# Attention's first steps in an order of their own, one expert's weights rounded a step later, the next expert's loads behind the last store of token rows

## Chip, cores and metric

The kernel runs on one core of one Trainium2 chip. The metric is device time in microseconds (us): 325.03 is the median of three runs, which lay between 324.36 and 325.7. Engines are abbreviated as in the profile: PE is TensorE (matmuls), PEld its weight loads, DVE VectorE, ACT ScalarE, POOL GpSimd, SP SyncE, which here only issues transfers. PEq, SPq and so on are the engines' instruction queues.

## Reference

Three layers run one behind the other on 2 batches of 768 tokens, all in 32-bit floats:

```python
# 1. attention with decay: 8 heads of 64; kv_state is carried along the sequence
out[:, :, sl] = ((qb @ kb.T) * Dmask) @ vb + (qb * lam_pow) @ kv_state
kv_state = lam_block * kv_state + (kb * rev_pow).T @ vb
...
# 2. mixture of 8 experts (512 -> 1024 -> 512), one expert for each token
logits = x @ w_gate
e = argmax(logits) if s == 0 or sigmoid(x @ w_local) < 0.5 else prev_e
out[b, s] = softmax(logits)[e] * (relu(x @ w1[e]) @ w2[e])
...
# 3. mixing: a causal depthwise filter of 5 taps gates a projection
gate = sigmoid(conv5(x, conv_w))
out = (gate * (x @ w_val)) @ w_out
```

A token that keeps its expert takes that of the token before it, so the choice runs along the sequence.

## The kernel before

**Attention** goes through 12 chunks of 128 tokens, 0 to 11, six of each batch. The instruction order of all engines is written out by hand in it (L534 to L690): a call such as `scores(2, 0)` issues its instructions on their engine at that place, and each engine then keeps that order. `load_qk` (L82) loads of chunk g, by SP, either the queries and keys for the scores (`qk0`, 512 KB) or the keys and values by token (`qk1`, 512 KB), or a half of one. On PE, `scores(g, half)` (L288) makes four heads' scores, `mix_state` (L309) multiplies queries with the carried state, `mix` (L321) scores with values, `next_state` (L350) makes the new state, `turned` (L370) turns the attention's result to rows of tokens and multiplies it with the gate's weights `wgl_sb`. On DVE, `mask` (L303) multiplies the scores with the decays `dm`; `keys_rest` (L281) and `keys` (L276) scale the keys, on DVE and on ACT; `queries` (L263) scales queries by powers `lq` that `powers` (L120) makes. `mixed` (L329) is ACT's copy of the result; `decay` (L335) and `keep_state` (L358) bring the state on. Ahead of all, `warm` (L529) multiplies zeros on PE.

The choice of the experts trails the attention by one to three chunks (`logits`, `choice`, `kept`, `experts`, `one_hots`, `counted`, `ranks`, `index_factors`, `indices`). `softmax(g)` (L430) ends a chunk: SP stores its 128 rows of 512 values and 8 softmax weights to `xd` in DRAM.

**The experts** run one after the other, 0 to 7. Every 32-bit weight is rounded to a part `whi` (ACT, `split_hi`, L194) and a rest `wlo` (DVE, `split_lo`, L199), and three of four products of parts are summed. Expert 0's eight weight tiles (four of `w1`, four of `w2`, 512 KB each) are loaded during attention by `load_next` (L186); the first four and a half are rounded in it by `first_hi` (L251) and `first_lo` (L256), in halves. The raw tiles, their parts and the `qk` tiles share one pool, `w4`, of 27 buffers. Expert 0's rows are placed by matmuls from what lies on the chip (`place`, L509; `early_split` rounds them), those of experts 1 to 7 are gathered from `xd`: `x_fetch` (L812) issues two indirect transfers of 128 rows on POOL, once `all_indices` (L699) has written the slots `idx`. Then `x_turn` (L828) turns each half on PE, `up` (L853) multiplies with `w1`, `down` (L870) with `w2`, and `down_few` (L880) does the few tokens above 128. In that time the matrices of layer 3, 64-bit values in the input, are loaded by `load64` (L233) and brought to 32 bits by DVE and POOL in `from64_a` (L208, its lines L217 to L226), one 512 KB tile beside each expert.

What the order around the change says of SP, at attention's end:

```python
        softmax(g0)
        load_next(4)
        load64(0)
...
        inverse(g1)
        softmax(g1)
        first_lo(4, HALF[1])
```

`g0` and `g1` are the last two chunks, 10 and 11. In the loop over the chunks before, rounding comes at step s as `first_hi((s - 3) // 2, HALF[(s - 3) % 2])` and `first_lo((s - 4) // 2, HALF[s % 2])`.

Of the kernel before, what the change touches and what calls it, by code (L numbers as in the profile page):

```python
# [44 lines left out]
def fused_kernel(ctx, tc, qkv, lam, wgl, w1, w2, wv, cw, wo, out, dbg=None):  # L45
# [58 lines left out]
    with tc.manual_schedule(engines={mybir.EngineType.SP, mybir.EngineType.DVE}):  # L104
        load_qk(0, slice(0, 1))
        load_qk(0, slice(1, 2))
        load_qk(1, slice(0, 2))
        load_qk(0, slice(2, 4))
        nc.sync.dma_start(wgl_sb, wgl)
        load_qk(1, slice(2, 4))  # L110
        load_qk(2, slice(0, 2))
        load_qk(2, slice(2, 4))
        nc.vector.memset(ones, 1.0)
        nc.vector.tensor_copy(ident16, ident)
        nc.vector.tensor_copy(identr, ident)

        for h in range(H):
            nc.vector.tensor_tensor_scan(dm[:, h, :], lam_sb[:, h:h + 1].to_broadcast([P, P]), last_first, 0.0,
                                         op0=MUL, op1=ADD)

    def powers():

        for hp in range(HP):
            nc.vector.tensor_tensor_scan(lq[:, hp, :], lam_sb[:, H + hp:H + hp + 1].to_broadcast([P, P]), ones, 1.0,
                                         op0=MUL, op1=MUL)
# [40 lines left out]

    nc.scalar.mul(thr_x, zero[:, 0:1], 1.0)
    nc.scalar.dma_start(xd[0:1, 0:XW].rearrange("o (a n) -> (o a) n", a=4), zero[0:4, 0:XW // 4])

# [117 lines left out]

    def scores(g, half, early=False):  # L288
        t = qk_t[g, 0]

        if half == 0 and early:
            rt = ps_1.tile([P, 2, HP, P], F32, name="rt", tag="rt")
            ps_t[g] = [rt[:, rh] for rh in range(2)]
        elif half == 0:
            ps_t[g] = [ps_s.tile([P, HP, P], F32, name=f"ps{rh}", tag=f"ps{rh}") for rh in range(2)]
        for hp in (2 * half, 2 * half + 1):
            for rh in range(2):
                r = slice(rh * 64, rh * 64 + 64)
                c0 = (hp % 2) * P
                nc.tensor.matmul(ps_t[g][rh][:, hp, :], t[r, half, 256 + c0:256 + c0 + P], t[r, half, c0:c0 + P],  # L300
                                 start=True, stop=True)

    def mask(g):  # L303
        ps = ps_t.pop(g)
        sm_t[g] = at_p.tile([P, 2, HP, P], F32, name="sm", tag="sm")
        for rh in range(2):
            nc.vector.tensor_tensor(sm_t[g][:, rh], ps[rh], dm[:, rh * HP:(rh + 1) * HP, :], op=MUL)

    def mix_state(g):  # L309
# [25 lines left out]
    def decay(g):  # L335
        if 0 < g % NC < NC - 1:
            sd_t[g] = sd = at_p.tile([P, HP, D], F32, name="sdec", tag="sdec")
            for hp in range(HP):
                nc.scalar.activation(sd[:, hp, :], state[g][:, hp, :], AF.Copy, scale=lq[:, hp, P - 1:P])
# [18 lines left out]
    def keep_state(g):  # L358
        if g in st_t:
            state[g + 1] = sn = at_p.tile([P, HP, D], F32, name="state", tag="state")  # L360
            if g % NC == 0:
                nc.vector.tensor_copy(sn, st_t.pop(g))
            else:
                nc.vector.tensor_tensor(sn, sd_t.pop(g), st_t.pop(g), op=ADD)
# [169 lines left out]
    with tc.manual_schedule(engines=order_a):  # L534
        warm(10)
        scores(0, 0)
        scores(0, 1)
        warm(6)
        mask(0)
        keys(0)  # L540
        load_qk(3)
        load_qk(4)
        scores(1, 0, True)
        scores(1, 1, True)
        mix_state(0)
        mix(0, 0)
        mix(0, 1)
        mixed(0)
        mask(1)
        keys_rest(0)  # L550
        powers()
        next_state(0)
        warm(2)
        keep_state(0)
        queries(1)
        keys(1)
        keys_rest(1)
        scores(2, 0)
        turned(0)
        for s in range(2, NT):  # L560
            g1, g2, g3 = s - 1, s - 2, s - 3
            last = s == NT - 1
            if s < NT - 3:
                load_qk(s + 3)
            if s in (2, 4, 6, 8):
                load_next()
# [30 lines left out]
            kept(g2)  # L597
            if 3 <= s < 11:
                first_hi((s - 3) // 2, HALF[(s - 3) % 2])
            keys(s, range(2))  # L600
# [10 lines left out]
            if last:  # L611
                softmax(g2)
                parts_hi(g2)
                first_hi(4, HALF[0])
            one_hots(g2)
            if last:
                first_hi(4, HALF[1])
            keys_rest(s)
            keys(s, range(2, HK))
            if s == NT - 2:  # L620
                softmax(g2)
            if s >= 4:
                first_lo((s - 4) // 2, HALF[s % 2])
            if g3 >= 0 and not last:
# [19 lines left out]
        place(ge, (0,))  # L644
        first_lo(4, HALF[0])
        experts(g0)
# [9 lines left out]
        softmax(g0)  # L656
        load_next(4)
        load64(0)
        place(ge, (1,))
        logits(g1)  # L660
        choice(g1)
        token_rows(g1)
        ranks(g0)
# [20 lines left out]
        softmax(g1)  # L684
        first_lo(4, HALF[1])
        place(g1)
        early_split()
        index_factors(ge)
        index_factors(g0)
# [663 lines left out]
```

## Time and profile before

| | before |
|---|---|
| median of three runs | 325.03 us (324.36 to 325.7) |
| the profiled execution | 324.66 us |
| its span, first to last instruction | 322.9 us |
| busy: PE, PEld, DVE, ACT, POOL | 97%, 86%, 81%, 64%, 27% |
| granted TensorE clock | 1.00 |
| memory traffic over the span | 225 GB/s |

The profile shows one execution. Its span leaves out 1.8 us around the first and the last instruction. A busy share is an average over attention (0 to about 75 us), experts (to about 250) and mixing, which have different limits. The chain of waits follows the work that ended last back to the start: it tells which engine's time the kernel consists of.

### The profile page before, as it was taken

The numbers are of one execution on the slowest core, as the hardware profiler recorded it, in microseconds if no ns is written. First come the engines' busy times: TensorE is split into PE (matmuls) and PEld (weight loads), VectorE is DVE, ScalarE is ACT, GpSimd is POOL, SyncE is SP. The second block draws the span as 40 slices with busy tenths as digits, with TensorE's granted clock in tenths as the row PEclk, the third lists the DMA queues.
The fourth block names the chain that finished last, engine by engine and source line by source line (L and its number), as shares of the span: only waits on it lengthen the run. The fifth ranks groups of instructions, "written<-read, shape, count | busy, mean of one in ns | idle before, by whom it ended". The sixth has DMA issues, their size and how long they took to land.

```text
span 322.9 us, 7304 instructions
## 1 busy us (share of the span) xinstructions
PE 314.0 (97%) x2714; PEld 276.8 (86%) x2714; DVE 261.0 (81%) x561; ACT 208.2 (64%) x519; POOL 87.3 (27%) x113
## 2 busy tenths in 40 slices
PE   8899999999979999999999999999999999999995
PEld 3688888889859889899798897988987989989984
DVE  5688899987968979959989799697756799977970
ACT  1589799976638646756576666865646666764741
POOL 7000000200645550550554516525234201020000
PEclk9999999999999999999999999999999999999999
DMA  7999899376599769599599399994304402221102
GB/s 214 376 406 318 298 376 292 150 205 256 180 295 368 285 222 384 202 294 367 215 316 399 120 361 366 304 400 155 96 20 129 125 26 73 102 90 66 63 37 106
DMA packets 27400, 73.09 MB, mean 226 GB/s; under 512 B 3799, under 2 KB 8157, under 8 KB 27357
## 3 DMA queue, kind: packets, MB, share of 16 engines
q1 hardware_dynamic: 24756, 65.09, 56.0%
q0 software_dynamic: 2304, 7.42, 7.5%
q8 instruction: 25, 0.41, 0.5%
q14 instruction: 19, 0.15, 0.1%
q10 hardware_dynamic: 296, 0.03, 0.1%
HBM read 57.79 MB, written 14.73 MB: 225 GB/s over the span
## 4 chain that ended last, share of the span: by engine, by line
PE 89%; DMA 5%; DVE 3%; ACT 1%; issue 1%; POOL 0%; SPq 0%; ACTq 0%
PE ph L862 24%; PE py L876 17%; PE pv L1021 11%; PE py L1047 10%; PE py L886 6%; PE ps L300 4%; PE po L326 3%; DMA xr<-xd,idx 3%; DMA qk<-in_qkv_dram 2%; PE rt L375 2%; PE po L318 2%; PE sp L355 1%; PE px L835 1%; PE rt L378 1%; PE rt L380 1%; PE pt L975 1%
## 5 line engine op out<-in xcount | busy, mean ns | idle before, releaser
L202 DVE TENSOR_TENSOR wlo<-wraw,whi 128x1024 fp32r<-128x1024 f32 (+1 forms) x69 | 85.4, 1264 | 12.9 <-ACT whi L197 12.9
L862 PE MATMUL ph<-xh,whi 128*128 128x240 f32 x512 | 87.2, 276 | 0.0
L862 PEld LDWEIGHTS ph<-xh,whi 128*128 128x128 f32 x512 | 77.4, 189 | 2.0 <-issue 1.5
L862 PE MATMUL ph<-xh,wlo 128*128 128x240 f32 x256 | 69.9, 274 | 0.0
L197 ACT CAST whi<-wraw 128x1024 fp32r<-128x1024 f32 (+1 forms) x69 | 65.3, 988 | 0.7 <-DVE wlo L202 0.7
L876 PE MATMUL py<-whi,hh 128*128 128x512 f32 x176 | 56.5, 392 | 0.0
L862 PEld LDWEIGHTS ph<-xh,wlo 128*128 128x128 f32 x256 | 48.4, 189 | 0.0
L1007 DVE SCALAR_TENSOR_TENSOR gt<-yt,cw_sb,gt 128x256 f32<-128x256 f32 x96 | 39.0, 481 | 1.1 <-ACT gt L999 1.1
L865 ACT ACTIVATE hh<-ph 128x480 fp32r<-128x480 f32 x32 | 18.3, 572 | 33.1 <-PE ph L862 32.7
L876 PEld LDWEIGHTS py<-whi,hh 128*128 128x128 f32 x176 | 33.1, 188 | 6.7
L1021 PEld LDWEIGHTS pv<-yh,wv_t 128*128 128x128 f32 x288 | 35.2, 192 | 0.7 <-ACT gt L999 0.4
L1021 PE MATMUL pv<-yh,wv_t 128*128 128x256 f32 x288 | 35.7, 284 | 0.0
L876 PE MATMUL py<-wlo,hh 128*128 128x512 f32 x88 | 34.4, 391 | 0.0
L1047 PE MATMUL py<-wo_t,gh 128*128 128x512 f32 (+1 forms) x156 | 34.1, 376 | 0.0
L226 POOL TENSOR_TENSOR f64a<-f64a,f64s 128x512 f32<-128x512 f32 (+1 forms) x9 | 18.2, 2027 | 55.6 <-DVE f64s L225 55.5
L1047 PEld LDWEIGHTS py<-wo_t,gh 128*128 128x128 f32 x156 | 27.4, 188 | 5.0
L867 DVE SCALAR_TENSOR_TENSOR hh<-ph,hh 128x480 fp32r<-128x480 f32 x32 | 20.9, 653 | 8.5 <-ACT hf L866 8.4
L815 POOL DMA_INDIRECT xr<-xd,idx x14 | 19.9, 1420 | 10.7 <-DVE hh L867 7.7
L876 PEld LDWEIGHTS py<-wlo,hh 128*128 128x128 f32 x88 | 16.5, 188 | 3.1
L886 PE MATMUL py<-wraw,hf 128*64 128x256 f32 x160 | 18.4, 382 | 0.0
L280 ACT ACTIVATE kd<-qk,dm 128x64 f32<-128x64 f32 x40 | 11.5, 343 | 7.8 <-DMA qk<-in_qkv_dram 7.8
L494 POOL DMA_INDIRECT xr<-xd,idx x2 | 2.1, 1052 | 52.0 <-ACT kp L443 51.7
(201 smaller groups left out, 516.4 us busy)
## 6 DMA issues: line engine op xcount, KB each, us to landing
wraw<-in_w_dram SPq DMA_DIRECT2D x64, 512.0 KB, 6.5
qk<-in_qkv_dram SPq DMA_DIRECT2D x23, 512.0 KB, 8.4
ys<-yo SPq DMA_DIRECT2D x16, 256.0 KB, 3.4
xd<-xtok SPq DMA_DIRECT2D x12, 260.0 KB, 3.6
ys<-warm_sb SPq DMA_DIRECT2D x24, 128.0 KB, 1.9
out_dram<-oo SPq DMA_DIRECT2D x11, 256.0 KB, 2.0
wraw<-in_w_val_dram SPq DMA_DIRECT2D x4, 512.0 KB, 6.6
wraw<-in_w_out_dram SPq DMA_DIRECT2D x4, 512.0 KB, 9.0
```

Of the source, the lines that this page charges most:

```text
L197: nc.scalar.copy(w[1][:, cs], w[0][:, cs])
L202: nc.vector.tensor_tensor(w[2][:, cs], w[0][:, cs], w[1][:, cs].bitcast(F32), op=SUB)
L226: nc.gpsimd.tensor_tensor(a.bitcast(F32), a.bitcast(F32), s.bitcast(F32), op=ADD)
L815: nc.gpsimd.indirect_dma_start(xr[:, t, :], None, xd, bass.IndirectOffsetOnAxis(ap=idx[:, 2 * e + t:2 * e + t + 1], axis=0))
L862: nc.tensor.matmul(ph[:, fi, :], w1_t[e][k][1 + a][:, f * P:(f + 1) * P], xh[b][:, k].rearrange("p t n -> p (t n)")[:, 0:C1], start=first, ...
L865: nc.scalar.activation(hh[:, 0, :, 0:C1], ph, AF.Relu)
L867: nc.vector.scalar_tensor_tensor(hh[:, 1, :, 0:C1], ph, 0.0, hh[:, 0, :, 0:C1].bitcast(F32), op0=ALU.max, op1=SUB)
L876: nc.tensor.matmul(py, hhs[f // 2][:, a, f % 2, t * P:(t + 1) * P], w2_t[e][f // 2][1 + b][:, (f % 2) * DM:(f % 2 + 1) * DM], start=(n == ...
L886: nc.tensor.matmul(py[i * NW:(i + 1) * NW, 0:DM // 2], hf[:, f, :], w2_t[e][f // 2][0][:, (f % 2) * DM + i * DM // 2:(f % 2) * DM + (i + 1 ...
L1007: nc.vector.scalar_tensor_tensor(gt[:, k, :], yt_t[b, k][:, c0 + j:c0 + j + 256], cw_sb[:, k, j:j + 1], gt[:, k, :], op0=MUL, op1=ADD)
L1021: nc.tensor.matmul(pv[:, mi, :], wv_t[:, a, k * DM + m * P:k * DM + (m + 1) * P], yh[b][:, k, :], start=first, stop=last)
L1047: nc.tensor.matmul(po, gh[a][:, k, t * P:(t + 1) * P], wo_t[:, b, k * DM + cs.start:k * DM + cs.stop], start=(i == 0), stop=(i == 11))
```

## The change

It has three parts. The first steps of attention are written out in another order, with chunk 0's values and keys loaded ahead of chunk 1's scores input, narrower masks for chunks 0 and 1 (`mask_half`), fewer warm-ups (8 and 3 in place of 10, 6 and 2), the first state copied by ACT, and chunk 1's state decayed by POOL. The rounding of expert 0's weights in the loop comes a step later. Expert 1's first four loads and the first 64-bit tile are issued behind the last `softmax`.

```diff
@@ loads ahead of the loop
         load_qk(0, slice(0, 1))
         load_qk(0, slice(1, 2))
+        load_qk(0, slice(3, 4))
+        load_qk(0, slice(2, 3))
         load_qk(1, slice(0, 2))
-        load_qk(0, slice(2, 4))
-        nc.sync.dma_start(wgl_sb, wgl)
         load_qk(1, slice(2, 4))
...
-    def powers():
-        for hp in range(HP):
+    def powers(hps):
+        for hp in hps:
...
+    nc.scalar.dma_start(wgl_sb, wgl)
...
+    def mask_half(g, half):
+        if half == 0:
+            sm_t[g] = at_p.tile([P, 2, HP, P], F32, name="sm", tag="sm")
+        hs = slice(2 * half, 2 * half + 2)
+        for rh in range(2):
+            nc.vector.tensor_tensor(sm_t[g][:, rh, hs], ps_t[g][rh][:, hs],
+                                    dm[:, rh * HP + 2 * half:rh * HP + 2 * half + 2, :], op=MUL)
...
     def decay(g):
         if 0 < g % NC < NC - 1:
             sd_t[g] = sd = at_p.tile([P, HP, D], F32, name="sdec", tag="sdec")
+            if g == 1:
+                nc.gpsimd.tensor_tensor(sd, state[g], lq[:, :, P - 1:P].to_broadcast([P, HP, D]), op=MUL)
+                return
...
     def keep_state(g):
...
-            if g % NC == 0:
+            if g == 0:
+                nc.scalar.copy(sn, st_t.pop(g))
+            elif g % NC == 0:
                 nc.vector.tensor_copy(sn, st_t.pop(g))
@@ the order
-        warm(10)
+        warm(8)
         scores(0, 0)
         scores(0, 1)
-        warm(6)
-        mask(0)
-        keys(0)
+        mask_half(0, 0)
+        mask_half(0, 1)
+        warm(3)
         load_qk(3)
         load_qk(4)
-        scores(1, 0, True)
-        scores(1, 1, True)
+        load_next()
+        powers((0, 1))
         mix_state(0)
         mix(0, 0)
         mix(0, 1)
         mixed(0)
-        mask(1)
         keys_rest(0)
-        powers()
+        keys(0)
+        powers((2, 3))
+        scores(1, 0)
+        scores(1, 1)
+        queries(1)
+        turned(0, (0, 1))
+        mask_half(1, 0)
+        mask_half(1, 1)
         next_state(0)
-        warm(2)
         keep_state(0)
-        queries(1)
+        turned(0, (2, 3))
         keys(1)
         keys_rest(1)
+        decay(1)
...
+        mix_state(1)
+        mix(1, 0)
+        mix(1, 1)
+        next_state(1)
...
         scores(2, 0)
-        turned(0)
-        for s in range(2, NT):
+        scores(2, 1)
...
+        for s in range(3, NT):
...
@@ rounding, in the loop
-            if 3 <= s < 11:
-                first_hi((s - 3) // 2, HALF[(s - 3) % 2])
+            if s > 3:
+                first_hi((s - 4) // 2, HALF[s % 2])
...
-                first_hi(4, HALF[0])
             one_hots(g2)
-            if last:
-                first_hi(4, HALF[1])
...
-            if s >= 4:
-                first_lo((s - 4) // 2, HALF[s % 2])
+            if s > 4:
+                first_lo((s - 5) // 2, HALF[(s - 5) % 2])
@@ behind the loop
         place(ge, (0,))
-        first_lo(4, HALF[0])
+        first_lo(3, HALF[1])
...
         softmax(g0)
-        load_next(4)
-        load64(0)
         place(ge, (1,))
         logits(g1)
         choice(g1)
+        first_hi(4, HALF[0])
...
         softmax(g1)
-        first_lo(4, HALF[1])
+        load_next(4)
+        load64(0)
+        first_lo(4, HALF[0])
         place(g1)
         early_split()
+        first_hi(4, HALF[1])
+        first_lo(4, HALF[1])
         index_factors(ge)
```

**SP, the first loads.** `qk_105` is chunk 0's scores input, in two halves. Before, `qk_108` is chunk 1's scores input and `qk_110` chunk 0's keys and values:

```order
L88 DMA qk_105<-in_qkv_dram 128x512 x2
L88 DMA qk_108<-in_qkv_dram 128x1024
L88 DMA qk_110<-in_qkv_dram 128x1024
L109 DMA wgl_sb<-in_wgl_dram 128x36
L88 DMA qk_113<-in_qkv_dram 128x1024
```

Now `qk_108` is chunk 0's values and keys and `qk_111` chunk 1's scores input:

```order
L88 DMA qk_105<-in_qkv_dram 128x512 x2
L88 DMA qk_108<-in_qkv_dram 128x512 x2
L88 DMA qk_111<-in_qkv_dram 128x1024
L88 DMA qk_113<-in_qkv_dram 128x1024
L88 DMA qk_115<-in_qkv_dram 128x1024
```

Chunk 1's scores input moves behind chunk 0's values and keys, and the gate's weights leave this queue.

**PE, from chunk 0's scores on.** The scores of chunk 1 stand ahead of the mixing (`po`) and state update (`sp`) of chunk 0 before:

```order
L300 MATMUL rt<-qk_108 128x128 x8
L326 MATMUL po<-sm,qk_110 64x128 x8
L355 MATMUL sp<-qk_110,kd 64x64 x8
L531 LDWEIGHTS warm_sb
L531 MATMUL pidx<-warm_sb 128x512
```

Now the mixing of chunk 0 comes first, then chunk 1's scores (`ps_243`, `ps_244`), then the turn and the state update:

```order
L332 MATMUL po<-sm,qk_108 64x128 x8
L298 MATMUL ps_243<-qk_111 128x128
L298 MATMUL ps_244<-qk_111 128x128
...
L386 MATMUL rt<-wid,xt 128x137 x2
L364 MATMUL sp<-qk_108,kd 64x64 x8
L389 MATMUL rt<-wgl_sb,xt 128x9
L391 MATMUL rt<-ident,xt 128x128
...
L324 MATMUL po<-qs,state 64x128 x8
L332 MATMUL po<-sm,qk_113 64x128 x8
L364 MATMUL sp<-qk_113,kd 64x64 x8
```

The mixing and state update of chunk 1 now follow at once, with chunk 2's scores behind them; two warm-ups between are gone.

**SP, the end of attention.** `xd` is the store of a chunk's rows, `wraw` a weight tile, `in_w_val_dram` the 64-bit matrix. Before, five loads stand ahead of the last store:

```order
L433 DMA xd<-xtok 128x520 x4
L191 DMA wraw<-in_w_dram 128x1024 x4
L237 DMA wraw_1373<-in_w_val_dram 128x1024
L433 DMA xd<-xtok 128x520
L237 DMA wraw_1688<-in_w_val_dram 128x1024
```

Now all five follow it:

```order
L444 DMA xd<-xtok 128x520 x5
L192 DMA wraw<-in_w_dram 128x1024 x4
L238 DMA wraw_1427<-in_w_val_dram 128x1024
L238 DMA wraw_1684<-in_w_val_dram 128x1024
L192 DMA wraw<-in_w_dram 128x1024 x4
```

The second 64-bit tile and the next four weight tiles stay behind them, in the same order.

## Rows read from the trace of the kernel before

**Rows 1.** The page, part 4: the chain that ended last, by engine.

```profile
PE 89%; DMA 5%; DVE 3%; ACT 1%; issue 1%; POOL 0%; SPq 0%; ACTq 0%
```

**Rows 2.** Chain of waits, 0 to 24 us: start us, us, what.

```profile
8.98 1.19 PE rt L300 x16
...
11.87 0.68 PE sp L355 x14
...
13.19 0.71 PE ps L300 x8
...
19.97 0.65 PE ps L300 x8
```

**Rows 3.** Timeline, 0 to 14 us: start, us, engine line op, tiles, count, [idle before].

```profile
1.26 4.45 PE L531 MATMUL pidx<-warm_sb 128*128 128x512 f16 x10 [1.26 <-DVE warm_sb L78]
...
7.11 1.47 PE L531 MATMUL pidx<-warm_sb 128*128 128x512 f16 x6
...
10.54 1.07 ACT L280 ACTIVATE kd<-qk,dm 128x64 f32<-128x64 f32 x4 [7.79 <-DMA qk<-in_qkv_dram]
```

**Rows 4.** Chain of waits, 72 to 116 us.

```profile
77.11 0.08 DVE idx L703
...
82.84 8.44 DMA xr<-xd,idx
...
95.47 10.95 PE ph L862 x96
...
111.93 0.64 PE px L835 x8
```

**Rows 5.** Timelines of POOL, 74 to 86, and PE, 88.9 to 92 us.

```profile
81.03 1.50 POOL L815 DMA_INDIRECT xr<-xd,idx  x1 [7.72 <-DVE hh L867]
...
89.25 0.46 PE L835 MATMUL px<-identr,xr 128*128 128x128 f32 x4
91.33 0.54 PE L835 MATMUL px<-identr,xr 128*128 128x128 f32 x4 [1.62 <-DMA xr<-xd,idx]
```

**Rows 6.** Timeline of SP, 66 to 74 us (issues, not transfers).

```profile
68.34 1.82 SPq L191 DMA_DIRECT2D wraw<-in_w_dram  x4
...
71.89 0.33 SPq L433 DMA_DIRECT2D xd<-xtok  x1
```

**Rows 7.** DMA issues at 3.1, 67.5, 68.3, 68.7, 71.8, 100.1 us: KB, us to landing.

```profile
qk<-in_qkv_dram SPq DMA_DIRECT2D x1, 512.0 KB, 8.6
...
xd<-xtok SPq DMA_DIRECT2D x1, 260.0 KB, 2.2
...
wraw<-in_w_dram SPq DMA_DIRECT2D x1, 512.0 KB, 4.6
...
wraw<-in_w_dram SPq DMA_DIRECT2D x2, 512.0 KB, 5.0
...
xd<-xtok SPq DMA_DIRECT2D x1, 260.0 KB, 8.4
...
xr<-xd,idx POOLq DMA_INDIRECT x1, 9.6
```

**Rows 8.** Timeline of DVE, 80 to 97 us.

```profile
81.62 0.42 DVE L217 TENSOR_SCALAR f64a<-wraw 128x512 uint32<-128x512 uint32 x1
...
90.36 0.69 DVE L837 TENSOR_TENSOR xh<-px,xh 128x512 fp32r<-128x512 f32 x1 [0.38 <-ACT xh L836]
...
93.13 2.16 DVE L202 TENSOR_TENSOR wlo<-wraw,whi 128x1024 fp32r<-128x1024 f32 x1
```

**Rows 9.** Line L226 over the run: min/median/max ns, first and last start.

```profile
L226 POOL TENSOR_TENSOR f64a<-f64a,f64s x9: 226/2207/4462, 92.9 to 237.1; 128x512 f32<-128x512 f32 x8, 128x20 f32<-128x20 f32 x1
```

**Rows 10.** Timelines of DVE and PEld, 74 to 76.2 us.

```profile
74.05 0.67 DVE L475 TENSOR_SCALAR ixa<-iotah,rk 128x256 f16<-128x256 f16 x3
...
75.44 0.22 PEld L481 LDWEIGHTS <-ixa 128*128 128x128 f16 x6
```

**Rows 11.** Windows: us, busy by engine (PE, PEld, DVE, ACT, POOL), PEclk, DMA share, GB/s.

```profile
89.70:91.30 1.60, 0.01 (x1) 0.00 (x0) 0.97 (x2) 0.58 (x1) 0.00 (x0) 1.00 1.00 332
```

More of the change, by code (lines that the diff above doesn't have):

```diff
@@ L115, in fused_kernel @@
         nc.vector.tensor_copy(identr, ident)
-        for h in range(H):
+        for h in (0, 1, HP, HP + 1, 2, 3, HP + 2, HP + 3):
             nc.vector.tensor_tensor_scan(dm[:, h, :], lam_sb[:, h:h + 1].to_broadcast([P, P]), last_first, 0.0,
                                          op0=MUL, op1=ADD)
-    def powers():
-        for hp in range(HP):
+    def powers(hps):
+        for hp in hps:
             nc.vector.tensor_tensor_scan(lq[:, hp, :], lam_sb[:, H + hp:H + hp + 1].to_broadcast([P, P]), ones, 1.0,
@@ L286, in keys_rest, with scores @@
                 dm[:, HK:H, P - 1:P].to_broadcast([P, H - HK, D]), op=MUL)
-    def scores(g, half, early=False):
+    def scores(g, half):
         t = qk_t[g, 0]
[L291 to L294, printed above, removed]
+        if half == 0:
             ps_t[g] = [ps_s.tile([P, HP, P], F32, name=f"ps{rh}", tag=f"ps{rh}") for rh in range(2)]
@@ L307, in mask @@
             nc.vector.tensor_tensor(sm_t[g][:, rh], ps[rh], dm[:, rh * HP:(rh + 1) * HP, :], op=MUL)
+    def mask_half(g, half):
+        if half == 0:
+            sm_t[g] = at_p.tile([P, 2, HP, P], F32, name="sm", tag="sm")
[3 more added lines that the diff above has]
+                                    dm[:, rh * HP + 2 * half:rh * HP + 2 * half + 2, :], op=MUL)
     def mix_state(g):
@@ L548, in fused_kernel @@
         mixed(0)
-        mask(1)
         keys_rest(0)
-        powers()
+        keys(0)
[6 more added lines that the diff above has]
+        mask_half(1, 1)
         next_state(0)
-        warm(2)
         keep_state(0)
-        queries(1)
+        turned(0, (2, 3))
         keys(1)
         keys_rest(1)
-        scores(2, 0)
-        turned(0)
-        for s in range(2, NT):
+        decay(1)
+        logits(0)
+        choice(0)
+        shift(0)
+        exponents(0)
+        token_rows(0)
+        mix_state(1)
+        mix(1, 0)
+        mix(1, 1)
+        next_state(1)
+        choice_turned(0, 1)
+        kept(0)
+        mixed(1)
+        queries(2)
+        scores(2, 0)
+        scores(2, 1)
+        keep_state(1)
+        experts(0)
+        mask(2)
+        load_qk(5)
+        inverse(0)
+        keys(2, range(2))
+        turned(1, (0, 1))
+        experts_turned(0)
+        turned(1, (2, 3))
+        scores(3, 0)
+        one_hots(0)
+        keys_rest(2)
+        keys(2, range(2, HK))
+        counted(0)
+        for s in range(3, NT):
             g1, g2, g3 = s - 1, s - 2, s - 3
@@ L564, in fused_kernel @@
                 load_qk(s + 3)
-            if s in (2, 4, 6, 8):
+            if s in (4, 6, 8):
                 load_next()
```

## The prediction

> **What bounds the kernel now.** I read the page first, then the chain of waits, then the timelines around the places where it leaves TensorE (PE), then the DMA issues. The chain's shares say that PE holds 89% of the span and single DMAs 5% [rows 1]. So work taken off other engines is worth nothing unless PE waits for it; what counts is where the chain leaves PE. It does so at two places that the change touches.
>
> The first is the start. PE begins the scores of chunk 1 at 8.98, when their input has landed, and from 13.19 it is on the chain without a gap: 6.78 us later, at 19.97, the second half of chunk 3's scores begins [rows 2]. ScalarE's (ACT's) first key instruction starts at 10.54, having waited for the load behind that one [rows 3].
>
> The second is the end of expert 0. The rows of expert 1 are fetched by two gathers. POOL could issue them once the indices exist (`idx`, at 77.11 + 0.08), but the first goes out at 81.03, the second at 82.84; PE turns the first half at 89.25, waits 1.62 us for the second gather and goes on at 91.33 [rows 4, 5]. POOL's row names VectorE's (DVE's) `hh` as the releaser, which was done long before; the true one is a DMA. SyncE's (SP's) queue shows it: five 512 KB loads go out from 68.34 on, and the last store of token rows at 71.89 behind them [rows 6]. That store took 8.4 us to land, where one issued on an emptier queue took 2.2 [rows 7]: 71.89 + 8.4 = 80.3, and the gathers need every store landed.
>
> **The change, part by part.** *The store ahead of the loads.* The store is issued when the softmax is ready, as before, and now has nothing ahead of it: it lands at 71.89 + 2.2 = 74.1. The gathers then start with the indices, at 77.2 in place of 81.03, the second 1.8 us after the first, at 79.0. Among loads, which is where they now run, a gather took as long as 9.6 us [rows 7]; so the second lands by 88.6, and PE wants it after 89.25. With no wait the two turns take 0.64 us, as for expert 2 [rows 4]; the next PE work starts at 89.25 + 0.64 = 89.89 and not at 91.33 + 0.54 = 91.87: **1.98 us saved**.
>
> What is late next? The five loads, now issued from 72.3, some 3.9 us later. The first took 4.6 us and landed at 72.95; the second, issued 0.45 later, took 5.4 (5.0 is the mean of the two) and landed at 74.2 [rows 6, 7]. At 1.25 us each the fifth came at about 78, and now comes at 82, or at 83.2 if the two gathers' 0.5 MB go between. DVE first reads it at 81.62 [rows 8], so DVE may stall up to 1.6 us, and behind it are queued the last `hh` of expert 0 and the rounding of expert 1's weights. DVE had idled 0.38 us before the first turned half [rows 8], so 1.2 of the 1.6 would be left. It delays the last weight part: without a stall that ends at 90.36 + 2 × 0.65 (the turned halves) + 2.16 = 93.8 [rows 8]; PE starts expert 1 at 95.47 − 1.98 = 93.49 and needs the part after nine matmuls of 10.95 / 96 = 0.11 us [rows 4], at 94.5. So 0.7 us of the 1.2 cost nothing and 0.5 would. I take 0, which any quicker loads give, and keep 0.5 as an end. The weight loads ahead of it are used by ACT from 84.6 on, over 2 us after the last.
>
> *The first steps.* The order of loads is now: the two scores halves of chunk 0, its values, its keys, then chunk 1's scores input. That input has 1 MB ahead of it in place of 0.5 MB, so it lands when the load that ACT waited for did: 10.5. From below its landing is bounded by 9.0, where the same transfer came with 0.5 MB ahead, from above by 3.15 + 8.6 = 11.75, where the load behind both came [rows 2, 7]. I take 10.5, since the bytes ahead are the same. From then on PE is to do chunk 1's scores (1.19), chunk 0's state update (0.68) and all that filled the 6.78 us, in another order [rows 2]; nothing else, as the mixing of chunk 0 now runs before. If nothing waits, that ends at 10.54 + 1.19 + 0.68 + 6.78 = 19.19 and not 19.97. Two waits could open: for ACT's copy of chunk 1's state, under which PE turns the second half of chunk 0, and for DVE's masks of chunk 1, under which PE turns chunk 0 and updates its state. I take 0.1 for both: **0.7 us saved**. At the ends, landing at 9.0 would save 2.2, at 11.75 it would lose 0.5.
>
> *The rest.* Chunk 1's decay on POOL: the same kind of pass over twice the size took 2.2 us, at worst 4.5 [rows 9], so 1.1 to 2.2 here; it starts when the state is there, at about 13.4, and the sum that wants it comes at about 15.7, after the mixing and the next state update: 0. The gate weights on ACT's queue go out earlier than on SP's: 0. Rounding a step later: eight half passes of ACT and of DVE stay, under steps that PE bounds; ACT's two in the last step go, 0 to 0.1 saved. The last DVE half pass (0.67) now runs ahead of the three index factors, which ended at 74.05 + 0.67 = 74.72; PE takes them at 75.44 [rows 10], 0.72 later: 0, at worst 0.1 lost.
>
> **Sum.** 324.66 − 1.98 − 0.7 = 321.98 on the profiled execution (span 322.9, 1.8 around it). That execution stood 0.37 under the median of the three runs, 325.03, so I forecast **322.3**.
>
> **A rule against it.** Between mixing chunk 0 and chunk 1's scores PE will idle for 1 to 1.6 us, after fewer warm-up matmuls. The rows show both levels of its clock: ten warm-ups at the start took 4.45 us, six later ones 1.47, so 0.445 and 0.245 each [rows 3]; the first ran at 1.2 GHz, the others at 2.4. The wait around 89.7 to 91.3 left the granted clock at 1.00, the upper level [rows 11]. The Trainium skill ("TensorE: Matmul & The Clock Gate", section "HAM oscillation — how this bites in real kernels") holds that bursts of matmuls parted by waits for DMA can each start at half clock again. By that rule, an estimate, the sum would be 324.9, for 2.6 us more (worked out below from the rows, as E); the trace does not bear it out for one wait of that length.
>
> **Rivals.** *A: both terms hold* (322.3), chance 0.62. For it: both waits stand on the chain, and behind them PE has no other until 111.
>
> *B: only the gather's term.* The input lands at 11.2 or later, where what follows no longer beats 19.97; two loads of 256 KB in place of one of 512 could do that. 325.03 − 1.98 = 323.05; with the landing at 11.75, 323.55. Against: the bytes ahead are the same. Chance 0.17. The Trainium skill ("DMA: Bandwidth & Descriptors", "Rules for kernel authors") wants transfers of 1 MiB and more, and its section "Anatomy of one DMA — SWDGE (gpsimd) path" gives each some 2 us of fixed cost; paid once more in series, an estimate, that would be a landing at 12.5 and 324.3. The rows show loads of 512 KB that take 4.6 and 5.4 us and land 1.25 apart, so what is fixed overlaps.
>
> *C: only the first steps' term.* The gathers now run beside the 2.5 MB of loads, not after them; if the second needs over 12 us, PE waits as before: 325.03 − 0.7 = 324.3. Against: 9.6 is the longest of the rows. Chance 0.10.
>
> *D: neither*, 325.0, chance 0.06: both of these at once.
>
> *E, slower: the clock falls at the wait ahead of chunk 1's scores.* At half clock PE's work takes twice as long, so half of the time that it stays low is lost. At the program's start it was low from 1.26 to somewhere between 5.7 and 7.1, some 5.2 us; that again costs 2.6 and gives 324.9. Low for all of the 8.6 us to 19.2 it costs 4.3: 322.3 + 4.3 = 326.6. It is slower than before from 5.4 us on. For it: the thinner start. Against: rows 11. Chance 0.05.
>
> **How the numbers follow.** A measurement of this kernel tells about 0.5% from no change, 1.6 us: faster is under 323.4, slower over 326.65. A is faster but for a sliver; of B, whose own range is 322.8 to 323.7, some 0.7; C and D are the same; E and a part of D are slower mostly. Faster 0.62 × 0.98 + 0.17 × 0.7 = 0.73; slower 0.04 + 0.02 = 0.06; same the rest, 0.21. The range: A alone reaches from 321.2 (the input at 9.8, and 0.4 between executions) to 323.2; B to 323.7; C's better half to 324.2. Half of C, D and E are left out, 0.16.
>
> **What would show it.** Right: the last store of rows lands some 2 us after its issue; POOL's first gather for expert 1 starts within 0.2 us of `idx`; PE has no wait at the turn of expert 1's rows; chunk 1's scores start near 10.5 and the second half of chunk 3's near 19.3, at a granted clock of 1.00. Wrong: DVE waiting for the fifth load so long that PE waits in expert 1's first matmuls; chunk 1's scores after 11.2; matmuls at the slow pace after 10 us; or the 2.7 us given back by a wait in a later expert, where PE now has none.

## The result, and the profile after

The changed kernel takes **320.75 us** (median of six runs, 320.41 to 321.69), the kernel before 324.69 us (six runs, 322.91 to 326.06): a ratio of 0.9892, 95% interval 0.9859 to 0.9926. It is faster by 3.9 us where 2.7 were forecast, and the median lies 0.45 us under the range. The profiled execution took 320.72 us, its span 319.0, against 324.66 and 322.9. Two slow runs of the experiments below, 612.25 us of z1_start_alone and 385.51 us of r1_fewer_warm, count in the medians and not in the ratios.

The page's chain of waits, by engine, shows where that went: DMA's share fell from 5% [rows 1] to 2%.

```profile
PE 93%; DVE 3%; DMA 2%; SPq 1%; ACT 0%; issue 0%; ACTq 0%
```

The chain's start (start us, us, what) answers to [rows 2]. Chunk 1's scores begin at 9.18, the second half of chunk 3's scores at 17.87 where it was 19.97: 2.10 us, three times the 0.7 forecast.

```profile
9.18 1.16 PE ps L298 x16
...
11.01 0.62 PE sp L364 x16
...
17.87 0.65 PE ps L298 x8
```

The chain around expert 0 answers to [rows 4]. Nothing but PE is on it. Expert 0 starts at 70.53, expert 1 at 91.57, 21.04 us later; before it was 95.47 less 72.61, 22.86 us. The wait at the turn of expert 1's rows [rows 5] is gone: 1.82 us.

```profile
70.53 2.99 PE ph L906 x24
...
87.33 0.64 PE px L879 x8
87.97 3.60 PE py L930 x32
91.57 10.95 PE ph L906 x96
```

POOL's timeline shows the gathers going out 0.4 us after `idx` (74.95 and 0.08), not 4 us after [rows 5]:

```profile
75.39 0.95 POOL L859 DMA_INDIRECT xr<-xd,idx  x1 [4.15 <-DVE cnt L757]
76.64 0.97 POOL L859 DMA_INDIRECT xr<-xd,idx  x1 [0.30 <-issue]
```

The last store, issued at 69.81, took 2.0 us to land where it had taken 8.4 [rows 7] (DMA issues, us to landing), and DVE waits 1.73 us for the 64-bit tile (its timeline), for which no PE instruction waits:

```profile
xd<-xtok SPq DMA_DIRECT2D x1, 260.0 KB, 2.0
```

```profile
81.36 0.43 DVE L218 TENSOR_SCALAR f64a<-wraw 128x512 uint32<-128x512 uint32 x1 [1.73 <-DMA wraw<-in_w_val_dram]
```

So far this reads as a right theory with one term too small. The experiments say that its two terms overlap.

### The profile page after: what moved, and what is told of

It is laid out like the page before. It is cut to its first block, busy times and chain, and to the rows that moved or that the text cites. A ratio compares the mean times of both kernels' runs of the same rounds, so it can differ in the third digit from the quotient of the medians.

```text
span 319.0 us, 7297 instructions
## 1 busy us (share of the span) xinstructions
PE 311.5 (98%) x2707; PEld 275.9 (86%) x2707; DVE 260.8 (82%) x564; ACT 207.2 (65%) x516; POOL 89.8 (28%) x114
## 4 chain that ended last, share of the span: by engine, by line
PE 93%; DVE 3%; DMA 2%; SPq 1%; ACT 0%; issue 0%; ACTq 0%
PE ph L906 27%; PE py L920 19%; PE pv L1065 11%; PE py L1091 10%; PE py L930 6%; PE ps L298 4%; PE po L332 3%; DMA qk<-in_qkv_dram 2%; PE rt L386 2%; PE po L324 2%; PE sp L364 1%; PE px L879 1%; PE rt L389 1%; PE rt L391 1%; PE pt L1019 1%; PE px L525 1%
## 5 line engine op out<-in xcount | busy, mean ns | idle before, releaser
L227 POOL TENSOR_TENSOR f64a<-f64a,f64s 128x512 f32<-128x512 f32 (+1 forms) x9 | 19.7, 2187 | 55.6 <-DVE f64s L226 55.6
L859 POOL DMA_INDIRECT xr<-xd,idx x14 | 19.3, 1378 | 7.2 <-DVE cnt L757 4.2
L298 PE MATMUL ps<-qk 64*128 64x128 f32 x192 | 16.5, 295 | 0.4 <-DMA qk<-in_qkv_dram 0.4
L930 PEld LDWEIGHTS py<-wraw,hf 128*64 128x64 f32 x160 | 11.0, 137 | 5.5
```

The source lines that it names most:

```text
L227: nc.gpsimd.tensor_tensor(a.bitcast(F32), a.bitcast(F32), s.bitcast(F32), op=ADD)
L859: nc.gpsimd.indirect_dma_start(xr[:, t, :], None, xd, bass.IndirectOffsetOnAxis(ap=idx[:, 2 * e + t:2 * e + t + 1], axis=0))
L930: nc.tensor.matmul(py[i * NW:(i + 1) * NW, 0:DM // 2], hf[:, f, :], w2_t[e][f // 2][0][:, (f % 2) * DM + i * DM // 2:(f % 2) * DM + (i + 1 ...
```

## The experiments

Each run's row gives its median, its ratio to the kernel before, and from PE's timeline of its profiled execution the first matmul of chunk 1's scores, of the second half of chunk 3's, and of expert 0, and the time from there to expert 1. "1 run" is a single time. Each ratio is to runs of the kernel before that were taken with it, so it differs a little from the ratio of the medians shown.

| run | median us | ratio (95%) | chunk 1 | chunk 3, half 2 | expert 0 | to expert 1 |
|---|---|---|---|---|---|---|
| before | 324.69 | 1 | 8.98 | 19.90 | 72.59 | 22.81 |
| the change | 320.75 | 0.9892 (0.9859 to 0.9926) | 9.18 | 17.80 | 70.52 | 20.98 |
| x1_store_first | 323.19 | 0.9977 (0.9947 to 1.0006) | 9.12 | 20.00 | 73.20 | 20.94 |
| z2_round_alone | 323.79 | 0.9991 (0.9956 to 1.0027) | 8.32 | 19.07 | 71.72 | 21.77 |
| z1_start_alone | 320.71 | 0.9894 (0.9864 to 0.9925) | 9.21 | 17.83 | 70.43 | 21.01 |
| x2_loads_ahead | 320.58 | 0.9895 (0.9865 to 0.9925) | 9.05 | 17.66 | 70.41 | 20.99 |
| x3_old_rounding | 320.39 | 0.9884 (0.9853 to 0.9916) | 9.04 | 17.66 | 70.22 | 20.99 |
| y1_gate_sp | 320.53, 1 run | | 8.99 | 17.61 | 70.34 | 20.94 |
| y2_one_load | 321.76, 1 run | | 9.93 | 18.54 | 71.29 | 21.01 |
| z3_one_load_again | 320.92 | 0.9903 (0.9870 to 0.9935) | 9.22 | 17.84 | 70.58 | 21.01 |
| y3_gate_act | 322.66, 1 run | | 8.26 | 19.01 | 71.70 | 21.70 |
| z4_gate_act_again | 323.14 | 0.9975 (0.9940 to 1.0009) | 8.77 | 19.51 | 72.90 | 21.91 |
| y4_halves | 324.34, 1 run | | 8.71 | 19.45 | 72.14 | 21.63 |
| r1_fewer_warm | 323.92 | 0.9985 (0.9956 to 1.0014) | 8.52 | 19.26 | 72.94 | 20.99 |
| r2_more_warm | 321.71 | 0.9922 (0.9897 to 0.9947) | 9.33 | 17.95 | 70.51 | 21.53 |
| r3_one_behind | 324.17, 1 run | | 9.04 | 21.16 | 73.86 | 20.99 |
| x4_rests_late | 320.59 | 0.9887 (0.9852 to 0.9922) | 9.12 | 17.73 | 70.30 | 20.98 |
| r4_best | 320.84 | 0.9882 (0.9851 to 0.9913) | 8.76 | 17.37 | 69.92 | 20.98 |

### The parts, alone and left out

**x1_store_first**: the kernel before with the loads moved and nothing else.

```diff
         softmax(g0)
-        load_next(4)
-        load64(0)
...
         softmax(g1)
+        load_next(4)
+        load64(0)
         first_lo(4, HALF[1])
```

> The kernel before, with nothing changed but the five loads, which go out behind the last store of token rows. Theory (the gathers were held by that store alone): the last store lands about 2 us after its issue, the first gather for expert 1 is issued within 0.3 us of idx, PE has no wait between the two turns of expert 1's rows, and expert 1 starts 1.98 us earlier than before (95.47, so 93.5); chunk 1's scores stay at 9.0. The time falls by 2.0, ratio 0.994. Rival (it helps only together with the new first steps): expert 1 starts at 95 or later, ratio 0.998 or more.

As the theory had it, the wait is gone, 20.94 us. The gain is smaller: the median fell by 1.4 against the runs beside it (324.62), the ratio stands for 0.7, and its interval reaches from 1.7 to no gain at all. The profiled execution, one of the slower ones (324.2), shows one reason: its expert 0 starts 0.6 us later than in the kernel before. ACT waited for a weight tile that it was to round in attention (the waits of ACT: us in total, times, longest), a wait that the profile of the kernel before does not have:

```profile
ACT whi L197 <- DMA wraw<-in_w_dram: 1.0, 2, 0.6
```

**x2_loads_ahead**: the changed kernel with the loads put back ahead of the last store (the diff above, reversed).

> The changed kernel with the five loads back ahead of the last store. Theory: the first steps' gain stays, the gathers' goes: chunk 1's scores start at 9.2, the second half of chunk 3's scores at 17.9, PE waits 1.5 to 2 us before the second half of expert 1's rows, and the kernel takes 2.0 us more than the changed one (320.75, so 322.7, ratio to before 0.9935). Rival (the two gains overlap): the time stays within 0.5 of 320.75.

The theory falls: 20.99 us, no wait, 320.58. **x3_old_rounding**, the changed kernel with the rounding calls of the kernel before:

> The changed kernel with the first expert's weights rounded at the steps where the kernel before rounds them. Theory A (the later rounding costs a little at attention's end, where from the second half of chunk 11's scores on the changed kernel takes 0.19 us longer to expert 0's first matmul than the kernel before, 13.61 for 13.44 from the same scores): expert 0 starts 0.2 us earlier than in the changed kernel (70.53, so 70.3), 320.55. Rival B (the later rounding saves 0.1, as predicted, or nothing): expert 0 starts at 70.5 to 70.7, 320.75 to 320.9. Rival C (chunk 3's step waits for the first weight tile, which lands only at 20.1): later by 0.5 or more.

Expert 0 starts 0.3 us earlier; 0.14 of it is there at chunk 3 already, so the rounding's part is some 0.16, near A. The median is 0.36 us lower, less than a measurement can tell. The next two complete the set. **z1_start_alone** undoes both at once, so that only the new first steps are left:

> The changed kernel with the five loads back ahead of the last store and the rounding at its old steps: the new first steps alone. Theory A (the gathers' wait hangs on chance differences of half a microsecond in when the last store lands, and on the rounding's order, which puts passes of DVE elsewhere): a wait of 0.5 to 2 us at the second half of expert 1's rows is back, expert 1 starts 21.6 to 22.8 us after expert 0, and the time is 321 to 322.5. Rival B (the new first steps alone take the wait away too): 21.0 us from expert 0 to expert 1, as in the changed kernel, and 320.4 to 320.8.

B holds. The new first steps alone give 320.71, all of the gain, with the five loads ahead of the store. The store is late there as well, landing 7.07 us after its issue, and the first gather goes out 7.21 us after expert 0's first matmul, where in the changed kernel it is 4.87; yet PE does not wait. **z2_round_alone** has the later rounding alone, on the kernel before:

> The kernel before with the rounding a step later and nothing else. Theory A (the rounding's order frees the gathers): 21.0 us from expert 0 to expert 1 instead of 22.8, and no wait of ACT for the first weight tile: 2 to 2.5 us under before, ratio 0.993. Rival B (it doesn't): 21.6 to 22.8 us, ratio 0.998 to 1.

No difference that can be measured, and the wait is there, 21.77 us: B. So the loads' move (x1) and the new first steps (z1, x2) each remove the same wait, and their gains don't add.

### When the first loads are whole

Chunk 1's scores input landed at 9.04, with 1 MB ahead of it, not at 10.5. Either the gate's weights, 128 pieces of 144 bytes on SP's queue before, had held the loads up, or the size of a load did. Four edits of two kernels, two of them run twice:

```diff
# y1_gate_sp, the changed kernel
         load_qk(1, slice(0, 2))
+        nc.sync.dma_start(wgl_sb, wgl)
...
-    nc.scalar.dma_start(wgl_sb, wgl)
# y2_one_load and z3_one_load_again, the changed kernel
-        load_qk(0, slice(3, 4))
-        load_qk(0, slice(2, 3))
+        load_qk(0, slice(2, 4))
# y3_gate_act and z4_gate_act_again, the kernel before
-        nc.sync.dma_start(wgl_sb, wgl)
...
+    nc.scalar.dma_start(wgl_sb, wgl)
# y4_halves, the kernel before
-        load_qk(1, slice(0, 2))
-        load_qk(0, slice(2, 4))
+        load_qk(1, slice(0, 1))
+        load_qk(1, slice(1, 2))
+        load_qk(0, slice(2, 3))
+        load_qk(0, slice(3, 4))
```

> The changed kernel with the gate's weights (128 pieces of 144 bytes) back on SP's queue, behind chunk 1's scores input. Theory G (these small pieces delay the loads that are in flight with them): chunk 1's scores start at 10 us or later, instead of 9.18. Rival S (it is the size of the pieces that sets when a load is whole: two loads of 256 KB come sooner than one of 512 KB): they start within 0.3 of 9.2. In both, the turn of chunk 0 may wait for the gate's weights.

> The changed kernel with chunk 0's keys and values in one load of 512 KB. Theory S (halves come sooner): mixing of chunk 0 starts at 9 or later, instead of 7.21, since it needs the whole, and chunk 1's scores at 10 or later, instead of 9.18. Theory G (the gate's small pieces): the load is whole at about 7.7, where its second half was, and chunk 1's scores start within 0.3 of 9.2.

> The kernel before with the gate's weights loaded from ACT's queue. Theory G: its third load, chunk 1's scores input, is whole at 7.7 or sooner instead of 8.94, chunk 0's keys and values at 9.0 instead of 10.5. Theory S: both within 0.3 of 8.94 and 10.5.

> The kernel before with its third and fourth load in halves of 256 KB. Theory S: the third is whole at 7.7 or sooner instead of 8.94, the fourth at 9.0 instead of 10.5. Theory G: both within 0.3 of 8.94 and 10.5.

> The changed kernel with chunk 0's keys and values in one load, a second time. Theory S (one load of 512 KB is whole later than two halves): chunk 1's scores start at 9.7 or later again, and the median is 0.7 to 1 us over the changed kernel's 320.75, so 321.5. Rival (chance between executions): they start at 9.0 to 9.2, and 320.75.

> The kernel before with the gate's weights loaded from ACT's queue, a second time. Theory G (on SP's queue, between the large loads, they hold up the third and fourth): chunk 1's scores start at 8.3 again, 0.7 earlier than before, the third load whole by 7, and the median is 0.7 to 1 us under before. Rival (chance): the third load is whole at 8.5 to 9 as in the kernel before, ratio 0.999 to 1.001.

y1 speaks against the gate's weights, though they stand behind chunk 1's scores input there. y3 and z4 seem to speak for them, y4 and y2 for the size; but z3 is y2 a second time and starts 0.7 us sooner, and z2, whose first loads are those of the kernel before to the last byte, shows the early landing too. The clearest row is ACT's wait for chunk 0's keys and values, the fourth load. In the kernel before it lasted 7.79 us [rows 3]; the waits of ACT in z2 have

```profile
ACT kd L280 <- DMA qk<-in_qkv_dram: 5.5, 1, 5.5
```

So executions of the same loads differ by over 2 us. The trace marks a load's end once for each sixteenth of it, and the load counts as landed with the last. In the kernel before, fourteen sixteenths of the third load were in by 6.70 and the other two came at 8.58 and 8.94; of the fourth, fourteen by 8.75, two at 9.99 and 10.46. x1, r1 and r3 (both below), whose first loads are unchanged as well, have late sixteenths too; their fourth load is whole at 10.56, 9.74 and 10.73. In z2, y3 and z4 no part is late: the third load is whole at 6.45 to 6.69, the fourth at 8.04 to 8.50. In the changed kernel and its variants x2, x3, x4, z1, y1 and r2 the fifth load, with the same bytes ahead of it as the fourth had before, is whole at 8.67 to 9.08 each time.

Chance is therefore not all. Sorted by size, the profiles say when chunk 0's inputs and chunk 1's scores input, 1.5 MB, were whole. With a third load of 512 KB it was after 9.7 in five of nine (before, x1, r1, r3 and y2: 9.74 to 10.73) and by 8.95 in four (z2, z3, y3, z4). With four loads of 256 KB first it was by 9.08 in all nine (the seven above, y4 and r4). Size in this weaker sense, as the odds of a late part, is left standing, and so are the gate's weights: of the kernels with the old first loads, four of the five with them on SP's queue were late and neither of the two without. With one profile each neither is shown, nor what makes a sixteenth late.

### What made the last store late

The wait for the gathers is in all five profiles that have the old first steps and the loads ahead of the store (before, z2, y3, z4, y4: 21.6 to 22.8 us to expert 1) and in neither of the two with the new ones (z1, x2). Its chain has three links. First, the store's last sixteenth: in the five it lands 0.65 to 1.53 us after the fifteenth, in z1 0.18 and in x2 0.46 after. Its last three pieces come late, right behind one 16 KB packet of an instruction queue. Here is 78.2 to 80.4 us of the kernel before, in 40 slices of 0.055 us, by what all DMA engines moved: the large packet in the first slice with two pieces of the store beside it, then nothing, then the three late pieces in slices 18, 22 and 26; below it the packet's queue (packets, MB, share of 16 engines' time: 2.6% of 2.2 us on 16 engines are 0.92 us on one).

```profile
GB/s 298 38 38 0 0 0 0 0 0 0 0 0 0 0 0 0 0 38 0 0 0 38 0 0 0 38 0 0 0 0 0 0 0 0 0 0 0 0 0 0
...
q8 instruction: 1, 0.02, 2.6%
```

The same view of z1, 76.0 to 78.2: the same packet, and no piece later than 0.28 us after its start.

```profile
GB/s 298 38 38 0 38 38 0 0 0 0 0 0 0 0 0 0 0 0 0 0 0 0 0 0 0 0 0 0 0 0 0 0 0 0 0 0 0 0 0 0
```

Is it this packet, a fetch of instructions by its queue's name? It starts 5.31 to 5.65 us after expert 0 in the five, 5.61 and 5.92 after in z1 and x2, which issue seven warm-ups (14 PE instructions) fewer. So two kernels move it by 12 PE instructions and leave every load and store where it was: **r1_fewer_warm** takes six warm-ups from the old first steps, **r2_more_warm** adds six to z1.

```diff
# r1_fewer_warm, the kernel before
-        warm(6)
# r2_more_warm, z1_start_alone
-        warm(3)
+        warm(9)
```

> The kernel before without its six warm-up matmuls behind chunk 0's scores: 12 PE instructions fewer, loads and stores as before. Theory I (a fetch of PE's instructions holds up the last pieces of the last store): the fetch comes 0.5 us later against expert 0's start (5.9 to 6.2 us behind it instead of 5.3 to 5.7), behind the store, whose last part lands within 0.5 us of the part before; the wait at expert 1's second half goes, and 21.0 us lie between the starts of expert 0 and 1. Theory B (bytes ahead of the store): 21.6 to 22.8 as before.

> The new first steps alone, with nine warm-up matmuls behind chunk 0's scores instead of three: 12 PE instructions more. Theory I: the fetch comes 0.5 us earlier against expert 0's start (5.1 to 5.4 us), in front of the store's last pieces on its engine, the store's last part lands 1 us or more behind the part before, and a wait of 0.5 to 2 us is back (21.6 us or more from expert 0 to expert 1). Theory B: 21.0 as with three. In both, chunk 1's scores start up to 0.7 us later.

The outcome is that of theory I both ways, the size of the shift is not. In r1 the packet comes 5.95 us after expert 0, the store's last part 0.11 us behind the fifteenth, and the wait is gone (20.99 us). In r2 it comes at 5.55, the last part 1.1 us behind the others, the wait is back (21.53), and the median is 1.0 us above z1's (0.5 between the two profiled executions). But 5.1 to 5.4 was expected, and 21.6 or more to expert 1: the packet of r2 starts only 0.06 us ahead of z1's 5.61, and in the kernel before it starts at 5.65, later than in z1, and the store is late. So its start against expert 0 alone does not decide. What all six profiles with a late store share is three pieces that start just when the packet's 0.92 us are over. The view of r1, 78.85 to 81.05, then of r2, 76.0 to 78.2, with the three late pieces in the same slices as in the kernel before:

```profile
GB/s 563 114 113 114 76 0 76 38 0 38 0 0 0 0 0 0 0 0 0 0 0 0 0 0 0 0 0 0 0 0 0 0 0 0 0 0 0 0 0 0
```

```profile
GB/s 38 411 38 38 76 38 38 76 38 0 0 0 0 0 0 0 0 38 0 0 0 38 0 0 0 38 0 0 0 0 0 0 0 0 0 0 0 0 0 0
```

r1's own time hardly moves, 323.92. Its profiled execution, too, has ACT waiting for a weight tile (1.1 us), and expert 0 at 72.94; and four of its ten runs have a mean granted clock of 0.992 or 0.993, near the 0.994 of r3 below. How much of the lost gain is due to each isn't shown.

The second link is POOL. Its two rows in r1 and in r2 (timelines):

```profile
80.60 0.95 POOL L814 DMA_INDIRECT xr<-xd,idx  x1 [6.95 <-DVE wlo L202]
81.86 1.01 POOL L814 DMA_INDIRECT xr<-xd,idx  x1 [0.30 <-issue]
```

```profile
78.94 1.50 POOL L859 DMA_INDIRECT xr<-xd,idx  x1 [7.72 <-DVE hh L911]
80.75 0.95 POOL L859 DMA_INDIRECT xr<-xd,idx  x1 [0.30 <-issue]
```

Begun 0.8 us later against expert 0, the first gather takes POOL 1.50 us to issue, not 0.95 (1.50 in the kernel before, 1.63 to 1.83 in y3, y4, z2 and z4). It is then held by a pass of DVE that makes the rest of a weight tile, `wlo` from `wraw` and `whi`. In the kernel before the gather begins at 81.03 [rows 5], during this pass (DVE's timeline):

```profile
80.49 1.22 DVE L202 TENSOR_TENSOR wlo<-wraw,whi 128x1024 fp32r<-128x1024 f32 x1
```

The pass ends at 81.71, the gather 0.82 us after it. Whether it began 8.10 or 8.44 us after expert 0, the first gather ends at 9.93 or 9.94 in all six. The same holds all along the eighteen profiles: the 151 gathers for experts that begin during such a pass end 0.81 to 0.94 us after its end and take up to 1.95 us, the other 137 take 0.94 to 1.17. The Trainium skill ("SBUF — State Buffer", "SBUF: two separate sides") says that POOL and DVE share a pair of ports, and that a DVE instruction with two inputs in SBUF, once it has begun, shuts out a POOL instruction that reads SBUF until it ends; the gather reads `idx`, and its end agrees.

The third is SP. In all six profiles with the wait the second gather goes out 10.24 or 10.25 us after expert 0, and SP's next five loads at 10.26 or 10.27. Beside them it takes 7.2 to 8.4 us; 1.35 us ahead of them it takes 4.2 in r1, 1.11 us ahead 4.8 in x2. The second and the third link are read from these traces; no run takes either of them out alone. From the DMA issues of r2 and of r1 (us to landing):

```profile
xr<-xd,idx POOLq DMA_INDIRECT x1, 7.2
```

```profile
xr<-xd,idx POOLq DMA_INDIRECT x1, 4.2
```

**r3_one_behind** moves one load of the five, the 64-bit tile, behind the store.

```diff
         softmax(g0)
         load_next(4)
-        load64(0)
...
         softmax(g1)
+        load64(0)
```

> The kernel before with one of the five loads, the 64-bit tile, behind the last store. Theory B (bytes ahead): the store lands 1.25 us earlier, about 6.3 us behind expert 0's start, the second gather goes out over 1 us before SP's next loads, and there is no wait: 21.0 us from expert 0 to expert 1. Theory I makes the same of it only if the fetch then falls behind the store; if the fetch is in front of its last pieces still, its last part lands 1 us behind the others, yet early enough: 21.0 to 21.5.

One load is enough: the store's last part lands 5.56 us after expert 0, the second gather goes out at 8.54, and there is no wait. Its time, a single run, is high for another reason, which brings back rival E of the prediction. In this execution the third load came at 9.00 and the fourth at 10.73, PE stood still from 7.61 to 9.04 and from 10.21 to 10.87, and its granted clock fell to the lower level. The windows (us, busy of PE, PEld, DVE, ACT and POOL, PEclk, DMA share, GB/s):

```profile
11.00:12.00 1.00, 1.00 (x14) 1.00 (x15) 1.00 (x3) 0.89 (x4) 0.29 (x2) 0.60 1.00 406
12.00:13.00 1.00, 1.00 (x20) 1.00 (x17) 1.00 (x4) 0.40 (x1) 0.00 (x0) 0.50 1.03 422
13.00:14.00 1.00, 1.00 (x10) 0.36 (x7) 0.70 (x3) 1.00 (x5) 0.00 (x0) 0.50 1.02 418
```

At 0.50, which is 1.2 GHz, chunk 3's second half begins at 21.16, 1.26 us after the kernel before. In r1 PE stood still for longer, from 6.00 to 8.52 and from 11.05 to 11.40, and the granted clock stayed at 1.00 in the profiled execution; so the length of the waits alone does not tell when it falls.

### Versions that were to beat both

**x4_rests_late** moves four half passes of DVE off attention's last steps.

```diff
-            if s > 4:
+            if 4 < s < 11:
                 first_lo((s - 5) // 2, HALF[(s - 5) % 2])
...
-        first_lo(3, HALF[1])
...
-        first_lo(4, HALF[0])
+        first_lo(3, HALF[0])
+        first_lo(3, HALF[1])
...
         first_hi(4, HALF[1])
-        first_lo(4, HALF[1])
         index_factors(ge)
         index_factors(g0)
         index_factors(g1)
+        first_lo(4, HALF[0])
+        first_lo(4, HALF[1])
```

> The changed kernel with four half passes of DVE (the rests of the fourth and fifth weight tile) moved behind the last softmax and behind the index factors. Theory: two of them, 0.60 us each, stand on the chain of waits in attention's last steps (61.2 and 64.0); without them expert 0 starts 0.6 to 0.85 us earlier (70.53, so 69.7 to 69.9), and the kernel takes 320.0. Rival: another engine ends there just behind DVE, or expert 0's first matmuls now wait for the fourth tile's rest, or its hidden rows queue behind the late passes on DVE: expert 1 starts at 91.57 or later, and the time is 320.75 or more.

0.2 us of the 0.6 came: ACT ends just behind DVE, as the rival says. **r4_best** moves ACT's three half passes as well and halves chunk 1's input:

```diff
-        load_qk(1, slice(0, 2))
+        load_qk(1, slice(0, 1))
+        load_qk(1, slice(1, 2))
...
-            if s > 3:
+            if 3 < s < 11:
                 first_hi((s - 4) // 2, HALF[s % 2])
...
-        first_hi(4, HALF[0])
+        first_hi(3, HALF[1])
...
         early_split()
-        first_hi(4, HALF[1])
+        first_hi(4)
```

> The changed kernel with the rests of the fourth and fifth weight tile moved as in x4, ACT's last three half passes moved likewise behind the choice of chunk 11 and behind the split of expert 0's rows, and chunk 1's scores input in two halves. Theory: PE's wait of 0.28 us for the counts at 61.4 goes and chunk 1's scores start 0.2 to 0.3 us sooner: expert 0 starts at 69.7 to 69.9 instead of 70.3, and the time is 320.0. Rival (PE finds the next wait at once, or expert 0's first matmuls wait for the late passes): 320.4 or more.

Expert 0 starts 0.6 us earlier than in the changed kernel, 0.43 of it at chunk 3 already, but the median, 320.84, is the same: these are differences that a measurement of this kernel can't tell. No version here beats the changed kernel measurably.

## Why the prediction was wrong

**The first steps** were mis-sized, at "I take 10.5, since the bytes ahead are the same". The order of work was right: from chunk 1's scores to chunk 3's second half the new order takes 8.62 us in the table (17.80 less 9.18), where the sum had 1.19 + 0.68 + 6.78 = 8.65. But the input came at 9.04, at the lower end, where the text has "would save 2.2"; 2.10 were measured. With that end the sum is 324.66 − 1.98 − 2.2 = 320.5, and 320.85 against the median. The 10.5 was the landing of another set of loads, two sixteenths of it late [rows 3], carried over by bytes alone. With the same bytes ahead the old loads came at 8.04 to 10.73 in seven profiles, the new at 8.67 to 9.08 in seven. Why the new loads were never as late stays open. The range failed with it: the text bounds the landing at 9.0, but the range begins at 9.8.

**The gathers** were right in size, 1.98 forecast and 1.82 measured, and half right in cause, at "the true one is a DMA". The loads do make the store late and hold the gathers, and the wait needs them, as x1 shows; but they are not enough, as z1 and x2 show. In the six profiles with the wait the store's last pieces also come behind a fetch of instructions, POOL issues the first gather slowly, and the second goes out with SP's next loads. With the new first steps, which have 14 PE instructions fewer, the store's late pieces are gone in z1 and x2. So the sum failed at "324.66 − 1.98 − 0.7", which adds two terms that overlap: the first steps alone give 3.8 us by the medians, the loads alone 1.4 (0.7 by the ratio, not clear of none), both 3.9. That the total came near to the two terms at their right size is luck as far as the parts go: the 1.82 would have come without the loads' move.

**The rounding** was forecast at 0 to 0.1, and is 0 as far as can be measured (z2). With the new first steps it costs about 0.15: from chunk 3 to expert 0 the table has 52.72 for the changed kernel and 52.56 for x3, 52.75 for x2 and 52.60 for z1. What the profile of before did not show is a wait of ACT for a weight tile, 1.0 to 1.2 us in x1, z4 and r1, all with the old first steps and the old rounding.

**The rest** held: the store at 2.0 us (2.2 forecast), DVE's stall of 1.73 us with nothing lost on PE ("I take 0"), a granted clock of 1.00 with the new first steps. Rival E's fall of the clock was seen, but on the other side: with the old first steps, in r3. Rival B's two loads of 256 KB in place of one of 512 cost nothing measurable (320.75 against z3's 320.92). Of the rivals none described what happened, since all took the two terms for independent.

**The kernel before is the wider one.** Its runs, taken with all of the experiments, lie between 321.4 and 326.9, the six of the change between 320.4 and 321.7. Late sixteenths, a late weight tile, the gathers' wait and the clock each cost 0.5 to 2 us in some profiles of it and its variants. One profile shows some of these and hides others.

## What to carry to other kernels

Before a term of a sum rests on when one transfer landed, look at its sixteen parts: if one or two are late, another execution may land 2 us sooner, and both ends belong in the forecast. Where a wait has several links, two edits that each break one link don't add, and an edit that has nothing to do with it, a few instructions more or fewer, can bring it back. Ask how far the wait is from going away by itself, and test a part alone and left out before you credit it.

## What the runs showed of the hardware

A fetch of instructions seems to hold up data. One 16 KB packet of an instruction queue takes 0.92 us, and in all six profiles with the wait the store's last three pieces start 0.90 to 0.91 us after it did, as if in line behind it; the trace does not name the DMA engine of a packet, so the shared engine is inferred. That the queue is PE's is an estimate from the profile page of the kernel before: the queue moves 25 such packets, 0.41 MB, which over PE's 2714 matmuls and 2714 weight loads is some 75 bytes each; the next engine, DVE, has 561 instructions. The Trainium skill ("Runtime: NRT & Kernel Launch", "Instruction fetch mechanics") describes such refills, in blocks of 16 KiB over a DMA queue of the sequencer's own, with a cost that is mostly hidden. For PE the traces agree, it has no wait beside the packet. For the store behind it the cost is not hidden: in the six profiles its last part lands 0.65 to 1.53 us behind the part before.

Another engine's pass can hold up a gather's issue: POOL took up to 1.95 us for one that began during DVE's `wlo` pass, and 0.94 to 1.17 otherwise.

The other surprise is that in r1 six warm-up matmuls less made the wait for a gather go away, over 80 us later, and in r2 six more brought it back.
